# Attention's first steps in a fused kernel: transposes of the first step ahead of the fourth step's scores, and the second pair's keys and queries loaded in two parts

## The chip, the cores and the metric

The kernel runs on one core of a Trainium2 chip. The metric is the device time of one execution in microseconds (us), the median of three timed runs. Everything below that is read from a trace comes from one profiled execution of the same program.

## What is computed

Attention over 2 batches, 8 heads, 768 positions and 64 columns per head, with a local window of 96 positions and 8 global ones, and then two feed-forward layers over the 1536 tokens. In the reference:

```python
scores = scale * np.matmul(q, k.transpose(0, 1, 3, 2)) + bias       # bias: -slope of the head * distance
scores = np.where(is_global | is_local, scores, -1000000000.0)
a = np.exp(scores - np.max(scores, axis=-1, keepdims=True))
a = a / (np.sum(a, axis=-1, keepdims=True) + 1e-09)
x = np.matmul(a, v)                  # laid out as 1536 tokens x 512
h = x @ w_in;  x = (h * np.tanh(softplus(h))) @ w_out               # first layer, 512 -> 2048 -> 512
h = x @ w_in2; return gate(h) @ w_out2                              # second layer, another gate
```

## The kernel before

Only attention's beginning is touched. `attention_windows` treats two heads at a time: a pair `(b, p)` is batch `b`, heads `2p` and `2p + 1`. Its keys `kr` (one copy of the window's keys per block of positions, `KB` = 144 columns each), queries `qr` and values `vr` are whole tiles in SBUF, loaded by `load_qk` and `load_v`. A pair has three steps of 256 positions each (`u` = 0 and 1 are the two blocks of 128); 8 pairs make `NU` = 24 steps, numbered `s` over all pairs. So steps 0, 1, 2 belong to pair (0,0) and steps 3, 4, 5 to pair (0,1), whose tiles are `kr01`, `qr01` and `vr01`.

One step is this chain: `scores(s)` on TensorE (PE), `softmax(s, u)` on VectorE (DVE: bias and maximum) and ScalarE (ACT: exponential and row sum), `normalise(s)` on DVE (two small operations) and GpSimd (POOL: four multiplications), `transposes(s)` on PE, `evict(s, 0)` on ACT and `evict(s, 1)` on DVE, which copy the transposed probabilities from PSUM, and `values(s)` on PE. The scores of odd and even steps lie in different PSUM banks, so `scores(s + 2)` can only begin when `softmax(s)` has read its banks.

The order on each engine is written by hand, and every engine runs its instructions in that order. The loop, once per `s`, software-pipelines the chain: in one turn PE gets `scores(s + 1)`, `transposes(s - 2)`, `values(s - 3)`, while DVE and ACT work on `softmax(s, 0)`, `normalise(s - 1)`, `evict(s - 2, 0)`, `softmax(s, 1)` and `evict(s - 2, 1)`. PE's turn for `s = 2` is thus `scores(3)` and then `transposes(0)`.

The loads stand in one queue, issued by the SyncE (SP) in the order of the code. Pair (0,0)'s keys and queries come ahead of everything, in two parts: the first 288 columns of the keys (`K0`) and 256 of the queries (`Q0`), which is what step 0 needs, and then the rest. Behind them come, in the version before, the whole of `kr01` and `qr01`, then `vr00`, `kr02`, `qr02`, `vr01`, `vr02`, and later pairs and weights. Each load has one of eight semaphores in turn, and an issue waits for the load that had that semaphore before, which is the one eight loads earlier.

Of the kernel before, what the change touches and what calls it, by code (L numbers as in the profile page):

```python
# [45 lines left out]
def attention_then_two_ffn_kernel(  # L46
# [29 lines left out]
    def half(j):  # L76
        return slice(j * D, (j + 1) * D)

    Q0, K0 = 2 * P, 2 * KB

    def load_qk(pool, b, p):

        kr = pool.tile([P, NB * KB], F32, tag="kr", name=f"kr{b}{p}")
        qr = pool.tile([P, S], F32, tag="qr", name=f"qr{b}{p}")
        if (b, p) == (0, 0):

            for cols in (slice(0, K0), slice(K0, NB * KB)):
                for j in range(2):
                    nc.sync.dma_start(kr[half(j), cols], k[b, p, half(j), j, cols])
                if cols.start == 0:  # L90
                    nc.sync.dma_start(qr[:, 0:Q0], q[b, p, :, 0:Q0])
            nc.sync.dma_start(qr[:, Q0:], q[b, p, :, Q0:])
        else:
            for j in range(2):
                nc.sync.dma_start(kr[half(j)], k[b, p, half(j), j])
            nc.sync.dma_start(qr, q[b, p])
        raws[b, p] = (qr, kr)

    def load_v(pool, b, p):
        vr = pool.tile([P, NSL, 2, D], F32, tag="vr", name=f"vr{b}{p}")  # L100
        nc.sync.dma_start(vr, v[b, p])
        return vr
# [5 lines left out]
    nc.sync.dma_start(raw, counts.partition_broadcast(P))  # L108
    first = ctx.enter_context(tc.tile_pool(name="first", bufs=1))
    load_qk(first, 0, 0)  # L110
    nc.scalar.preload_act_table_set("natural_log_exp_and_others")
    WU = 2 * DM
# [55 lines left out]
    def rounded(on, to, src):  # L168
        if on == "a":
            nc.scalar.activation(to, src, AF.Copy)  # L170
        else:
            (nc.vector if on == "v" else nc.gpsimd).tensor_copy(to, src)  # L172

    def remainder(on, to, src, hi):
        (nc.vector if on == "v" else nc.gpsimd).tensor_tensor(to, src, hi.bitcast(F32), op=ALU.subtract)  # L175
# [129 lines left out]
    def attention_windows(x_hi, x_lo, bank, wts, opening):  # L305
        with ExitStack() as es:
            cp = es.enter_context(tc.tile_pool(name="a_const", bufs=1))
            rp = es.enter_context(tc.tile_pool(name="a_raw", bufs=3))
            pp = es.enter_context(tc.tile_pool(name="a_p", bufs=2))
            sp = es.enter_context(tc.tile_pool(name="a_s", bufs=3))  # L310
            vs = {}
            for p in range(3):
                if p < 2:
                    load_qk(rp, 0, p + 1)
                vs[0, p] = load_v(rp, 0, p)
            bias = cp.tile([P, H, 3 * P], F32, name="bias")

# [16 lines left out]
            NU = len(steps)  # L334
# [3 lines left out]
            def scores(s):  # L338
                b, p, t = steps[s]
                qr, kr = raws[b, p]  # L340
                scs[s] = [bank(SC[s % 2][j], [2, 2 * P]) for j in range(2)]
                for u in range(2):
                    i = 2 * t + u
                    for j, ps in enumerate(scs[s]):
                        nc.tensor.matmul(ps[:, u, 0:keys(i)], qr[half(j), i * P:(i + 1) * P],  # L345
                                         kr[half(j), window(i):window(i) + keys(i)], start=True, stop=True)

            def softmax(s, u):
                b, p, t = steps[s]
                if u == 0:  # L350
                    probs[s] = (pp.tile([P, 2, 2, 2 * P], F32, tag="pr", name=f"pr{s}", bufs=3),
                                sp.tile([P, 2, 2, 4], F32, tag="st", name=f"st{s}", bufs=3))
                pr, st = probs[s]
                n = keys(2 * t + u)
                for j, ps in enumerate(scs[s]):
                    h = 2 * p + j
                    nc.vector.tensor_tensor_reduce(  # L357
                        pr[:, u, j, 0:n], ps[:, u, 0:n], bias[:, h, 0:n] if n > P else bias[:, h, 2 * P:],
                        scale=-scale, scalar=3e38, op0=ALU.add, op1=ALU.min,
                        accum_out=st[:, u, j, 0:1],  # L360
                    )
                    nc.scalar.activation(pr[:, u, j, 0:n], pr[:, u, j, 0:n], AF.Exp, scale=-1.0,  # L362
                                         bias=st[:, u, j, 0:1], accum_out=st[:, u, j, 1:2])

            def normalise(s):
                pr, st = probs[s]
                nc.vector.tensor_scalar(st[..., 2], st[..., 1], 1e-9, None, op0=ALU.add)
                nc.vector.reciprocal(st[..., 3], st[..., 2])  # L368
                for u in range(2):
                    n = keys(2 * steps[s][2] + u)  # L370
                    for j in range(2):
                        nc.gpsimd.tensor_scalar(pr[:, u, j, 0:n], pr[:, u, j, 0:n], st[:, u, j, 3:4], 1.0,  # L372
                                                op0=ALU.mult, op1=ALU.mult)

            def blocks(s):

                t = steps[s][2]
                return [(u, j, o) for u in range(2) for j in range(2) for o in range(keys(2 * t + u) // P)]

            def transposes(s):  # L380

                pr = probs.pop(s)[0]
                pts[s] = (pp.tile([P, 8, P], F32, tag="pts", name=f"pts{s}"), [bank(TR[c], [8, D]) for c in range(2)])
                for n, (u, j, o) in enumerate(blocks(s)):
                    for c, pt in enumerate(pts[s][1]):
                        nc.tensor.transpose(pt[:, n], pr[half(c), u, j, o * P:(o + 1) * P], ident[half(c), half(c)])  # L386

            def evict(s, c):
                n = len(blocks(s))
                dst, src = pts[s]  # L390
                rounded("av"[c], dst[:, 0:n, half(c)], src[c][:, 0:n])

            def values(s):
                b, p, t = steps[s]
                vr = vs[b, p]
                src = pts.pop(s)[0]
                place = {x: n for n, x in enumerate(blocks(s))}
                for u in range(2):
                    i = 2 * t + u
                    g, (t0, n) = [(g, x) for g, x in enumerate(pieces) if x[0] <= i * P < x[0] + x[1]][0]  # L400
                    pv = bank(PV[g], [n])
                    m = keys(i) // P
                    for o in range(m):
                        for j in range(2):
                            nc.tensor.matmul(pv[half(j), i * P - t0:(i + 1) * P - t0], vr[:, 2 * i - m + 1 + o, j],  # L405
                                             src[:, place[u, j, o]], start=(o == 0), stop=(o == m - 1))
                    if (i + 1) * P == t0 + n:
                        done.append((x_hi[b][:, p, t0:t0 + n], x_lo[b][:, p, t0:t0 + n], pv))
# [3 lines left out]
            for s in range(-1, NU + 4):  # L412

                if s in (3, 7):
                    wts.load()
                if s >= 2 and s % 3 == 2 and s // 3 + 3 < len(pairs):
                    load_qk(rp, *pairs[s // 3 + 3])
                if s >= 6 and s % 3 == 0 and s // 3 + 1 < len(pairs):
                    vs[pairs[s // 3 + 1]] = load_v(rp, *pairs[s // 3 + 1])
                ready, done[:] = done[:], []  # L420
                for hi, lo, src in ready:
                    rounded("a", hi, src)
                if s + 1 < NU:
                    scores(s + 1)
                if 0 <= s - 2 < NU:
                    transposes(s - 2)
                if 0 <= s - 3 < NU:
                    values(s - 3)
                if 0 <= s < NU:
                    softmax(s, 0)  # L430
                if 0 <= s - 1 < NU:
                    normalise(s - 1)
                for hi, lo, src in ready:
                    remainder("v", lo, src, hi)
                if 0 <= s - 2 < NU:
                    evict(s - 2, 0)
                if 0 <= s < NU:
                    softmax(s, 1)
                if 0 <= s - 2 < NU:
                    evict(s - 2, 1)  # L440
                for name in BESIDE.get(s, ()):
                    opening[name]()
                    if name in ("V01", "V11"):
                        wts.load()
# [612 lines left out]
    with tc.If(few != 0) as cmp:  # L1057
        arm(attention_windows, True)
# [53 lines left out]
```

## Time and profile before

| | |
|---|---|
| median of three runs | 603.69 us (603.65 to 604.11) |
| the profiled execution | 604.59 us |
| its span, first to last instruction | 602.8 us |
| PE busy | 585.0 us (97%) |
| DVE busy | 464.4 us (77%) |
| ACT busy | 398.5 us (66%) |
| attention's steps, about | 5 to 80 us of the span |

The span is what the trace shows; 1.79 us of the profiled execution lie outside it. The shares of busy time are means over attention and the two layers, which have different limits: in attention PE, DVE and ACT are all nearly full, in the layers PE alone is. The change lies wholly in the span's first 20 us. Times below are counted from the span's start.

### The profile page before, as it was taken

To read this page: it belongs to the slowest core of one execution; us is meant where nothing else is said; L and a number is where in the kernel's file an instruction comes from. 1 tells how busy PE (TensorE), PEld (TensorE's weight loads), DVE (VectorE), ACT (ScalarE), POOL (GpSimd) and SP (SyncE) were. 2 spreads that over 40 slices of the span, in tenths; PEclk is the share of its full clock that TensorE was granted. 3 is DMA by queue.
4 is the path that set the end of the run, shared out by engine and by line. 5 is a ranking of instruction groups with operands and counts; after the bars stand their busy time and mean duration, and the time that the engine had idled before them with its cause. 6 is when DMAs were issued, how large, how long until landed. Compare 5 with 4: busy or idle time off the path is not lost.

```text
span 602.8 us, 9716 instructions
## 1 busy us (share of the span) xinstructions
PE 585.0 (97%) x3536; PEld 512.4 (85%) x3536; DVE 464.4 (77%) x1036; ACT 398.5 (66%) x872; POOL 67.3 (11%) x146
## 2 busy tenths in 40 slices
PE   5998999999999999999999999999999999999996
PEld 3887789999999999999999888878888888888884
DVE  6999998888888676776767774988688787787571
ACT  4999978888888566677766876667464643544240
POOL 3776710000000000000000000000020140200000
PEclk9999999999999999999999999999999999999998
DMA  7998024433334202221535566510042270310012
GB/s 197 297 272 247 32 71 140 140 103 114 134 141 139 71 1 70 71 82 60 183 114 192 152 194 214 149 61 2 0 126 84 64 216 1 111 29 0 1 47 99
DMA packets 17335, 66.64 MB, mean 111 GB/s; under 512 B 2176, under 2 KB 2432, under 8 KB 13184
## 3 DMA queue, kind: packets, MB, share of 16 engines
q1 hardware_dynamic: 11808, 55.98, 29.6%
q0 software_dynamic: 4608, 8.39, 4.9%
q10 hardware_dynamic: 864, 1.57, 0.7%
q8 instruction: 30, 0.49, 0.3%
q14 instruction: 25, 0.20, 0.1%
HBM read 54.40 MB, written 11.53 MB: 109 GB/s over the span
## 4 chain that ended last, share of the span: by engine, by line
PE 87%; DVE 7%; ACT 3%; DMA 1%; SPq 1%; issue 0%; POOL 0%; DVEq 0%
PE psum L591 22%; PE psum L895 14%; PE psum L805 13%; PE psum L541 10%; PE psum L542 10%; PE psum L544 10%; PE psum L600 7%; DVE pr L357 2%; ACT pr L362 2%; PE psum L345 1%; DVE pts L172 1%; DVE x_lo L175 1%; PE psum L386 1%; PE psum L405 1%; DMA qr<-in_q_dram 1%
## 5 line engine op out<-in xcount | busy, mean ns | idle before, releaser
L541 PE MATMUL psum<-x_hi,whi 128*128 128x384 f32 (+1 forms) x320 | 111.2, 348 | 0.4 <-DVE kr L558 0.4
L542 PE MATMUL psum<-x_lo,whi 128*128 128x384 f32 (+1 forms) x320 | 110.6, 346 | 0.0
L591 PE MATMUL psum<-g_lo,whi 128*128 128x512 f32 (+1 forms) x256 | 86.6, 338 | 0.1
L591 PE MATMUL psum<-g_hi,wlo 128*128 128x512 f32 (+1 forms) x256 | 86.2, 337 | 0.0
L591 PE MATMUL psum<-g_hi,whi 128*128 128x512 f32 (+1 forms) x256 | 86.1, 336 | 0.0
L544 PE MATMUL psum<-x_hi,wlo 128*128 128x384 f32 (+1 forms) x320 | 71.8, 345 | 0.0
L541 PEld LDWEIGHTS psum<-x_hi,whi 128*128 128x128 f32 x320 | 60.2, 188 | 3.7 <-DVE kr L558 0.6
L170 ACT ACTIVATE whi<-wbits 128x512 fp32r<-128x512 f32 x72 | 44.5, 618 | 27.6 <-DVE wbits L758 14.1
L542 PEld LDWEIGHTS psum<-x_lo,whi 128*128 128x128 f32 x320 | 60.2, 188 | 2.4
L544 PEld LDWEIGHTS psum<-x_hi,wlo 128*128 128x128 f32 x320 | 57.3, 188 | 2.5
L175 DVE TENSOR_TENSOR wlo<-wbits,whi 128x512 fp32r<-128x512 f32 x76 | 51.9, 689 | 9.2 <-ACT whi L170 9.1
L731 POOL DMA_DIRECT2D whi<-kept_hi x16 | 8.7, 541 | 430.4 <-ACT room_lo L844 362.5
L591 PEld LDWEIGHTS psum<-g_lo,whi 128*128 128x128 f32 x256 | 48.2, 188 | 5.8 <-DVE g_lo L580 0.5
L591 PEld LDWEIGHTS psum<-g_hi,whi 128*128 128x128 f32 x256 | 48.2, 188 | 5.7
L591 PEld LDWEIGHTS psum<-g_hi,wlo 128*128 128x128 f32 x256 | 48.1, 188 | 5.7
L362 ACT ACTIVATE pr<-pr,st 128x256 f32<-128x256 f32 (+1 forms) x96 | 46.0, 482 | 8.4 <-DVE st L357 8.2
L227 ACT ACTIVATE wbits<-stage 128x512 uint16<-128x512 uint16 x64 | 50.0, 782 | 0.7 <-DVE wlo L175 0.7
L372 POOL TENSOR_SCALAR pr<-pr,st 128x256 f32<-128x256 f32 (+1 forms) x96 | 44.4, 480 | 27.9 <-DVE st L368 14.4
L234 DVE SCALAR_TENSOR_TENSOR wbits<-wsc,wbits 128x512 uint32<-128x512 uint32 x60 | 41.5, 691 | 6.8 <-ACT wbits L227 2.5
L345 PE MATMUL psum<-kr,qr 64*128 64x256 f32 (+1 forms) x192 | 31.3, 413 | 10.8 <-DVE wsc L151 5.3
L162 ACT ACTIVATE wsc<-stage 128x512 f32<-128x512 f32 x60 | 39.6, 660 | 0.0
L357 DVE CUSTOM_DVE_ANT_0 pr<-psum,bias 128x256 f32<-128x256 f32 (+1 forms) x96 | 34.0, 393 | 1.2 <-PE psum L345 1.2
(158 smaller groups left out, 1284.3 us busy)
## 6 DMA issues: line engine op xcount, KB each, us to landing
stage<-in_w_dram SPq DMA_DIRECT2D x32, 1024.0 KB, 5.0
vr<-in_v_dram SPq DMA_DIRECT2D x8, 704.0 KB, 10.7
kept_hi<-whi SPq DMA_DIRECT2D x8, 512.0 KB, 7.2
kept_lo<-wlo SPq DMA_DIRECT2D x8, 512.0 KB, 8.0
whi<-kept_hi POOLq DMA_DIRECT2D x16, 256.0 KB, 3.8
wlo<-kept_lo POOLq DMA_DIRECT2D x16, 256.0 KB, 3.9
kr<-in_k_dram SPq DMA_DIRECT2D x14, 216.0 KB, 12.6
qr<-in_q_dram SPq DMA_DIRECT2D x7, 384.0 KB, 11.7
```

The source lines that it names most:

```text
L170: nc.scalar.activation(to, src, AF.Copy)
L175: (nc.vector if on == "v" else nc.gpsimd).tensor_tensor(to, src, hi.bitcast(F32), op=ALU.subtract)
L227: nc.scalar.activation(bits[:, i, :, 0], words(U16, i, 1), AF.Copy, scale=2.0 ** -13, bias=2.0 ** -14 - 0.5)
L357: nc.vector.tensor_tensor_reduce(pr[:, u, j, 0:n], ps[:, u, 0:n], bias[:, h, 0:n] if n > P else bias[:, h, 2 * P:], scale=-scale, scalar=3 ...
L362: nc.scalar.activation(pr[:, u, j, 0:n], pr[:, u, j, 0:n], AF.Exp, scale=-1.0, bias=st[:, u, j, 0:1], accum_out=st[:, u, j, 1:2])
L372: nc.gpsimd.tensor_scalar(pr[:, u, j, 0:n], pr[:, u, j, 0:n], st[:, u, j, 3:4], 1.0, op0=ALU.mult, op1=ALU.mult)
L541: nc.tensor.matmul(ph, wh[:, c], xh[:, c, tok], start=(c == 0), stop=False)
L542: nc.tensor.matmul(ph, wh[:, c], xl[:, c, tok], start=False, stop=False)
L544: nc.tensor.matmul(ph, wl[:, c], xh[:, c, tok], start=False, stop=(c == KD - 1))
L591: nc.tensor.matmul(y, lhs[:, w], rhs[:, t0:t0 + n], start=(f == 0 and i == 0 and c % share == 0), stop=(f == NF - 1 and i == 2 and c % sha ...
L805: nc.tensor.matmul(ps, a[:, cols], x, start=(n == 0), stop=(n == 3 * HK - 1))
L895: nc.tensor.matmul(ys[c], lhs[:, w], rhs, start=(n == 0 and k == 0), stop=(n == len(fs) - 1 and k == 2))
```

## The change

The transposes of step 0 are taken out of their place behind `scores(3)` and issued ahead of it. Pair (0,1)'s keys and queries are loaded in two parts, as the first pair's are: first columns, then `vr00`, then the rest. Nothing is computed otherwise, and no later turn of the loop differs.

```diff
-    def load_qk(pool, b, p):
+    def load_qk(pool, b, p, between=None):
 
         kr = pool.tile([P, NB * KB], F32, tag="kr", name=f"kr{b}{p}")
         qr = pool.tile([P, S], F32, tag="qr", name=f"qr{b}{p}")
-        if (b, p) == (0, 0):
+        if (b, p) == (0, 0) or between:
 
             for cols in (slice(0, K0), slice(K0, NB * KB)):
                 for j in range(2):
                     nc.sync.dma_start(kr[half(j), cols], k[b, p, half(j), j, cols])
                 if cols.start == 0:
                     nc.sync.dma_start(qr[:, 0:Q0], q[b, p, :, 0:Q0])
+                    if between:
+                        between()
             nc.sync.dma_start(qr[:, Q0:], q[b, p, :, Q0:])
...
             vs = {}
-            for p in range(3):
-                if p < 2:
-                    load_qk(rp, 0, p + 1)
+            def first_values():
+                vs[0, 0] = load_v(rp, 0, 0)
+
+            load_qk(rp, 0, 1, first_values)
+            load_qk(rp, 0, 2)
+            for p in range(1, 3):
                 vs[0, p] = load_v(rp, 0, p)
...
                 for hi, lo, src in ready:
                     rounded("a", hi, src)
+                if s == 2:
+                    transposes(0)
                 if s + 1 < NU:
                     scores(s + 1)
-                if 0 <= s - 2 < NU:
+                if 0 < s - 2 < NU:
                     transposes(s - 2)
```

TensorE, in the version before, from the last scores of pair (0,0) on. `kr_68` and `qr_69` are that pair's tiles, `kr_166` and `qr_167` pair (0,1)'s; `pr_193` and `pr_207` are the probabilities of steps 0 and 1, and `vr_171` is `vr00`.

```order
L345 MATMUL psum<-kr_68,qr_69 128x256 x10
L345 MATMUL psum<-kr_166,qr_167 128x128 x2
L345 MATMUL psum<-kr_166,qr_167 128x256 x2
L386 MATMUL psum<-ident,pr_193 128x64 x12
L345 MATMUL psum<-kr_166,qr_167 128x256 x4
L386 MATMUL psum<-ident,pr_207 128x64 x16
L405 MATMUL psum<-pts_234,vr_171 64x128 x6
```

The same place with the change (the lines of the code are moved by five; `pr_196` and `pr_210` are the probabilities of steps 0 and 1).

```order
L350 MATMUL psum<-kr_68,qr_69 128x256 x10
L391 MATMUL psum<-ident,pr_196 128x64 x12
L350 MATMUL psum<-kr_166,qr_167 128x128 x2
L350 MATMUL psum<-kr_166,qr_167 128x256 x6
L391 MATMUL psum<-ident,pr_210 128x64 x16
L410 MATMUL psum<-pts_233,vr_171 64x128 x6
```

The twelve transposes of step 0 moved from behind the four products of `scores(3)` to ahead of them, and the four products of `scores(4)` now follow those of `scores(3)` at once.

SyncE's queue of loads, before, from the first load of pair (0,1) on (`kr_173` and `qr_174` are pair (0,2)'s, `vr_178` and `vr_180` are `vr01` and `vr02`).

```order
L95 DMA kr_166<-in_k_dram 64x864 x2
L96 DMA qr_167<-in_q_dram 128x768
L101 DMA vr_171<-in_v_dram 128x1408
L95 DMA kr_173<-in_k_dram 64x864 x2
L96 DMA qr_174<-in_q_dram 128x768
L101 DMA vr_178<-in_v_dram 128x1408
L101 DMA vr_180<-in_v_dram 128x1408
```

The same place with the change (`kr_176` and `qr_177` are pair (0,2)'s now).

```order
L89 DMA kr_166<-in_k_dram 64x288 x2
L91 DMA qr_167<-in_q_dram 128x256
L103 DMA vr_171<-in_v_dram 128x1408
L89 DMA kr_166<-in_k_dram 64x576 x2
L94 DMA qr_167<-in_q_dram 128x512
L97 DMA kr_176<-in_k_dram 64x864 x2
L98 DMA qr_177<-in_q_dram 128x768
```

Three loads became six; the second parts of `kr01` and `qr01` stand behind the 704 KB of `vr00` instead of ahead of them, and `kr02` and all behind it stand three issues later.

## Rows read from the trace of the kernel before

**Rows 1.** The page's head and its first part, TensorE's row.

```profile
span 602.8 us, 9716 instructions
...
PE 585.0 (97%) x3536; PEld 512.4 (85%) x3536; DVE 464.4 (77%) x1036; ACT 398.5 (66%) x872; POOL 67.3 (11%) x146
```

**Rows 2.** Busy time in 16.0 to 25.6 us: PE, PEld, DVE, ACT, POOL, clock, DMA.

```profile
16.00:25.60 9.60, 9.41 (x132) 8.16 (x134) 9.32 (x44) 9.60 (x38) 8.00 (x18) 1.00 1.03 320
```

**Rows 3.** Timeline of PE: start, length, line, tiles, count, idle time before, releaser.

```profile
7.83 3.78 PE L345 MATMUL psum<-kr,qr 64*128 64x256 f32 x16 [0.86 <-DMA qr<-in_q_dram]
12.89 1.02 PE L345 MATMUL psum<-kr,qr 64*128 64x128 f32 x8 [1.28 <-DVE st L367]
...
14.12 1.08 PE L345 MATMUL psum<-kr,qr 64*128 64x256 f32 x7
14.91 0.78 PE L386 MATMUL psum<-ident,pr 64*128 64x64 f32 x16
15.92 0.88 PE L405 MATMUL psum<-pts,vr 128*64 128x128 f32 x12 [0.23 <-DMA vr<-in_v_dram]
16.72 1.27 PE L345 MATMUL psum<-kr,qr 64*128 64x256 f32 x8
17.69 0.85 PE L386 MATMUL psum<-ident,pr 64*128 64x64 f32 x16
...
27.29 0.93 PE L345 MATMUL psum<-kr,qr 64*128 64x128 f32 x8
```

**Rows 4.** Timeline of SP's queue: when each load was issued.

```profile
6.96 0.58 SPq L96 DMA_DIRECT2D qr<-in_q_dram  x1
7.59 0.43 SPq L101 DMA_DIRECT2D vr<-in_v_dram  x1
8.06 1.11 SPq L95 DMA_DIRECT2D kr<-in_k_dram  x2
9.22 1.26 SPq L96 DMA_DIRECT2D qr<-in_q_dram  x1
...
15.89 0.33 SPq L96 DMA_DIRECT2D qr<-in_q_dram  x1
```

**Rows 5.** Loads issued at 2.44, 4.22, 6.96, 7.59, 15.89: KB, us to landing.

```profile
qr<-in_q_dram SPq DMA_DIRECT2D x1, 128.0 KB, 2.4
...
qr<-in_q_dram SPq DMA_DIRECT2D x1, 256.0 KB, 3.5
...
qr<-in_q_dram SPq DMA_DIRECT2D x1, 384.0 KB, 5.8
...
vr<-in_v_dram SPq DMA_DIRECT2D x1, 704.0 KB, 8.3
...
qr<-in_q_dram SPq DMA_DIRECT2D x1, 384.0 KB, 10.5
```

**Rows 6.** Timeline of DVE, 11 to 15 us.

```profile
11.57 0.08 DVE L357 DVE_READ_ACCUMULATOR2_ANT st<- 128x1 f32 x1
...
12.49 0.35 DVE L367 TENSOR_SCALAR st<-st 128x4 f32<-128x4 f32 x1
...
14.31 0.56 DVE L172 COPY pts<-psum 128x384 f32<-128x384 f32 x1 [0.60 <-PE psum L386]
```

**Rows 7.** Timeline of POOL: the last multiplication of step 0, all four of step 1.

```profile
12.34 0.47 POOL L372 TENSOR_SCALAR pr<-pr,st 128x256 f32<-128x256 f32 x1
...
13.28 1.83 POOL L372 TENSOR_SCALAR pr<-pr,st 128x256 f32<-128x256 f32 x4
```

**Rows 8.** Timeline of ACT: evictions of steps 0, 1, 2, and what precedes the first.

```profile
13.67 0.19 ACT L362 ACTIVATION_READ_ACCUMULATOR pr<-pr,st 128x1 f32 x1
14.26 0.49 ACT L170 ACTIVATE pts<-psum 128x384 f32<-128x384 f32 x1 [0.41 <-PE psum L386]
...
16.40 0.58 ACT L170 ACTIVATE pts<-psum 128x512 f32<-128x512 f32 x1
...
18.85 0.58 ACT L170 ACTIVATE pts<-psum 128x512 f32<-128x512 f32 x1
```

## The prediction

> **What bounds the kernel now.** I read the page's head and the busy times first: the span is 602.8 us and TensorE (PE) is busy for 97% of it [rows 1]. That share is a mean over stages, so I went on to the busy time by stretches. From 16.0 to 25.6 us ACT is busy for all 9.60 us, PE for 9.41 and DVE for 9.32, at the full granted clock, and the DMA engines are full too [rows 2]. Nothing has room there: whatever delays one engine at the start of attention is carried along, and whatever frees all three is kept. So the change is worth what it shifts ACT, the fullest, and nothing that it does later can add to it.
>
> Then the timeline of the place. PE stands idle for 1.28 us ahead of `scores(3)`, which begin at 12.89, and the profile puts this down to a DVE operation at 12.49 [rows 3, 6]. I don't believe the name. What `scores(3)` needs of DVE is that it has read the scores of step 1, and that ended with the reading at 11.57 (0.08 long) [rows 6]; the operation at 12.49 is the next step's. The queries of pair (0,1) were issued at 6.96 and landed 5.8 us later, at 12.76 [rows 4, 5], and PE starts 0.13 us after that. It is the same distance as at the first pair: issued at 4.22, 3.5 us to landing, PE at 7.83 [rows 3, 5]. So `scores(3)` wait for a load, and `transposes(0)`, which stand behind them, wait with them. For those transposes ACT is idle for 0.41 us before 14.26 and DVE for 0.60 before 14.31 [rows 6, 8]. A third wait, of 0.23 us at 15.92, is PE's for `vr00`: 7.59 plus 8.3 is 15.89 [rows 3 to 5].
>
> **The change part by part.** All sums are made against the profiled execution (span 602.8, whole 604.59), which is 0.9 us over the median of 603.69; I apply the difference to both.
>
> *Transposes first.* They need step 0's probabilities from POOL, whose last multiplication starts at 12.34 and takes 0.47 us [rows 7], so it ends at 12.81. Twelve transposes cost, by the sixteen that take 0.78 us [rows 3], 0.05 us each; eight of them can go earlier, the last four follow 12.81, and with some 0.2 us for the pipeline they are done at about 13.25. ACT comes free at 13.86 (13.67 + 0.19) [rows 8], DVE at 14.31 - 0.60 = 13.71 [rows 6]. Both find the transposes done. So ACT's 0.41 us and DVE's 0.60 us go away. What is moved costs nothing: PE would have stood idle. `scores(3)` start at about 13.1 instead of 12.89, and this is hidden, as their first reader on DVE stands behind the eviction that takes 13.71 to about 14.2.
>
> *First columns in front.* They are 72 KB twice and 128 KB, and the nearest row, the first pair's 128 KB, landed in 2.4 us [rows 5]: issued at 6.96, here at 9.4. At worst they land with the whole tile at 12.76. Either is ahead of 13.1, when `scores(3)` can first start behind the transposes. So the first part by itself is worth nothing: the transposes have already taken the place of the wait. `vr00` has 544 KB fewer ahead of it and lands at some time before 15.89, which takes up to 0.23 us of PE's wait away.
>
> *The second part behind `vr00`.* This is what is late next. `scores(4)` read columns 176 to 432 of the keys and 256 to 384 of the queries, so they need the second parts, which before lay whole in SBUF at 12.76. Now three issues take the slots at 8.06 to 9.22 that `kr02` and `qr02` had [rows 4], and 544 KB go behind the 704 KB. When does the last of them, issued at 9.22, land? The earliest is its quickest precedent, 256 KB in 3.5 us [rows 5]: 12.7. The latest is 15.89, the landing of `vr00` in the version before, since the bytes in the queue up to there are the same. In between I have no row that decides; both ends are whole precedents, so I take the middle, 14.3.
>
> What it costs follows from the steady turn. From landing to start 0.1 us; `scores` to `transposes` of a turn without waits 17.69 - 16.72 = 0.97; the sixteen transposes 0.79 (16.72 + 0.97 + 0.79 is where the values of that turn begin) [rows 3]. So ACT's eviction of step 1 can begin at landing + 1.86. Before, it began at 16.40 [rows 8], and with ACT 0.41 earlier it would at 15.99. It is therefore early by the full 0.41 when the second part lands by 14.1, and even at 14.54. PE has less room: `values(0)` begin at landing + 1.86 instead of 15.92, and the eviction of step 2, at 18.85 before [rows 8], needs `values(0)`, `scores(5)` and `transposes(2)`, which took from 15.92 to about 18.53 (17.69 + 0.85) [rows 3], a reserve of 0.3 us. So the shift at 18.85 is landing + 1.86 - 15.92 - 0.32, that is landing - 14.38, and no better than -0.41. With 14.3 it is -0.1 us. With 12.7 it is -0.41; with 15.89 it is +1.5.
>
> *What is queued behind.* While `scores(4)` wait, `transposes(1)`, `values(0)` and `scores(5)` wait behind them on PE, and for these ACT and DVE; that is the sum above. On SP, three more issues push `kr02` back by about 1.7 us (0.58 each [rows 4]), but the DMA engines are full, so bytes and not issues set when it lands. An issue also waits for the load eight ahead of it: `vr02` now waits for `vr00`, and the keys of pair (0,3) behind it. Before, its queries were the load that waited for `vr00`, issued at 15.89 and landed 10.5 us later, at 26.4; `scores(9)` used them at 27.29 [rows 3 to 5]. They now wait for the second part of `qr01`, not later than 15.89. Reserve 0.9 us, so nothing.
>
> The sum: -0.41 from the transposes, +0.3 back through `scores(4)`, so about -0.1 us: 604.5 for a profiled execution, 603.6 for the median.
>
> **The rivals.**
>
> *Wholly hidden.* The second part lands by 14.0 and the change gives its 0.41 us, at best the 0.57 that PE can have (`values(0)` from 15.92 to 15.35, POOL's last multiplication of step 1 ending at 13.28 + 1.83 = 15.11 [rows 7]). The median is then 603.1 to 603.3. For it speaks the precedent of 3.5 us; against it, that this one was the last load in a short queue, while now 704 KB lie ahead. The Trainium skill (DMA: Bandwidth & Descriptors, on the two cost components of a transfer) gives about 2.0 us and the bytes at 436 GB/s, which would be an estimate of 2.6 us and a landing at 11.8, hidden with ease; the row of 3.5 us for the same size is already longer, and 5.8 and 8.3 us behind it show that a queue is not in that rule.
>
> *The other side: the second part lands behind all of `vr00`.* For it speaks that the loads of rows 5 landed in the order of issue, 12.76 and then 15.89, each after the bytes ahead of it. If it lands at 15.6 or later, the shift is over +1.2 us and the change is slower; at 15.89 the median is 605.2. Against it, that the second part is small, and that 12.76 to 15.89 held other loads as well. The Trainium skill (same page, on HWDGE ordering) says that each DMA engine takes its descriptors in ring order and that a load is complete only when every engine has done its share; by that the second part cannot pass `vr00`, which the order of the landings bears out.
>
> *The change gains much more.* Over 1.2 us would need all of PE's 1.28 us; POOL's 12.81 and 15.11 forbid it.
>
> *A later load becomes late*, through the eight semaphores or the smaller pieces. Only the reserve of 0.9 us at 27.29 could go, some 0.5 us slower.
>
> **How the numbers follow.** The forecast (landing between 14.0 and 15.0, shift -0.4 to +0.6) has 0.55; wholly hidden 0.25; behind all of `vr00` 0.12, with 15.0 to 15.6 counted to the forecast's side; a later load 0.05; much more 0.03. The likeliest shift is -0.1 us, so 603.6. A measurement of this kernel can tell 0.2% from no change, 1.2 us: only landings after 15.6 reach it on one side, and nothing that I can work out on the other. So faster 0.03, same 0.85, slower 0.12. The range goes from the hidden case with 0.1 us for the spread of the runs, 603.1, to the middle of the late one, 604.9.
>
> **What would show it right or wrong.** Right: `transposes(0)` end at 13.0 to 13.3 and evictions begin at 13.7 to 13.9; `scores(3)` begin at 13.1; ahead of `scores(4)` or behind them PE waits for a `qr` or `kr` load, and this sets the evictions of step 1. The load of 256 KB issued at about 9.2 shows its landing. From 16 us on every engine's rows are shifted by one amount, and the layers behind show none of their own. Wrong: a landing before 13 or after 15.9; an eviction of step 1 that is early although the load was late; a shift that shrinks or grows after 20 us, which would mean that the stretch there is not as full as I read it.

## The result, and the profile after

The change makes the kernel slower: 608.41 us, the median of six runs (607.62 to 609.12), against 604.19 for the version before in the same measurement (603.65 to 606.07); the ratio is 1.0065, 95% interval 1.005 to 1.008. The forecast was 603.6 with a range up to 604.9, so the result lies outside it, on the side that I gave 0.12. The profiled execution of the changed kernel took 609.0 us, the second longest of the six; its span is 607.2, 4.4 more than [rows 1], where the medians differ by 4.2. The code's lines are moved by two to seven: the scores are L350 here, the transposes L391, the values L410, the evictions of ACT L172.

First the head of the page of the changed kernel, and the row of TensorE's clock in 40 slices of the span.

```profile
span 607.2 us, 9720 instructions
...
PEclk9799999999999999999999999999999999999999
```

One slice stands out: in the second, about 15 to 30 us, the granted clock was 0.7 of full speed on average. The same row before had no such slice. Next the timeline of PE in the changed kernel, to be laid beside [rows 3].

```profile
7.44 3.79 PE L350 MATMUL psum<-kr,qr 64*128 64x256 f32 x16 [0.41 <-DMA qr<-in_q_dram]
11.22 1.60 PE L391 MATMUL psum<-ident,pr 64*128 64x64 f32 x12
12.65 0.95 PE L350 MATMUL psum<-kr,qr 64*128 64x128 f32 x8
16.49 2.17 PE L350 MATMUL psum<-kr,qr 64*128 64x256 f32 x8 [2.88 <-DMA qr<-in_q_dram]
18.33 1.18 PE L391 MATMUL psum<-ident,pr 64*128 64x64 f32 x16
19.44 1.55 PE L410 MATMUL psum<-pts,vr 128*64 128x128 f32 x12
20.91 1.66 PE L350 MATMUL psum<-kr,qr 64*128 64x256 f32 x8
22.41 0.66 PE L391 MATMUL psum<-ident,pr 64*128 64x64 f32 x16
```

`transposes(0)` and `scores(3)` are where I put them, a little earlier still. Then PE stands idle for 2.88 us ahead of `scores(4)`, for a load of queries. The load is the 256 KB of `qr01`'s second part; its issue in SP's queue:

```profile
9.22 0.59 SPq L94 DMA_DIRECT2D qr<-in_q_dram  x1
```

and from the DMA issues of these windows what the values (issued at 7.58) and this second part took from issue to landing:

```profile
vr<-in_v_dram SPq DMA_DIRECT2D x1, 704.0 KB, 5.7
...
qr<-in_q_dram SPq DMA_DIRECT2D x1, 256.0 KB, 7.1
```

The values landed at 13.28, earlier than before (15.89, [rows 4, 5]), and the second part at 16.36 by the chain of waits (9.22 and 7.14): later than either end of my bounds. The busy times of the changed kernel by stretches (PE, PEld, DVE, ACT, POOL, granted clock, DMA share, GB/s):

```profile
13.40:15.00 1.60, 0.21 (x2) 0.00 (x0) 0.96 (x6) 1.60 (x7) 1.33 (x3) 1.00 1.09 196
15.00:16.40 1.40, 0.00 (x0) 0.00 (x0) 0.87 (x6) 0.59 (x4) 0.99 (x3) 0.57 1.02 209
16.40:21.60 5.20, 5.11 (x40) 4.53 (x42) 1.89 (x8) 2.15 (x8) 1.34 (x3) 0.50 1.05 345
21.60:24.00 2.40, 2.40 (x40) 2.00 (x36) 1.36 (x6) 1.24 (x4) 2.12 (x5) 0.91 0.99 180
```

While PE waited, its clock fell from 2.4 to 1.2 GHz, at about 15.2 us, and it stayed there until about 22.0 (0.91 as the mean of the last row), through nearly all of the work that had been waiting. The same view of 8 to 16 us in one stretch, first of the changed kernel, then of the one before:

```profile
8.00:16.00 8.00, 5.39 (x36) 3.53 (x32) 6.30 (x37) 7.39 (x30) 4.53 (x11) 0.95 1.02 240
```

```profile
8.00:16.00 8.00, 6.50 (x62) 5.24 (x64) 5.49 (x31) 6.93 (x28) 3.92 (x9) 1.00 1.00 269
```

The DMA engines are as full in both, and move less in the changed kernel. And the evictions of ACT, of steps 0 to 3, beside [rows 8]:

```profile
13.37 0.47 ACT L172 ACTIVATE pts<-psum 128x384 f32<-128x384 f32 x1
19.45 0.60 ACT L172 ACTIVATE pts<-psum 128x512 f32<-128x512 f32 x1 [3.86 <-PE psum L391]
...
23.16 0.60 ACT L172 ACTIVATE pts<-psum 128x512 f32<-128x512 f32 x1 [1.16 <-PE psum L391]
...
26.10 0.48 ACT L172 ACTIVATE pts<-psum 128x384 f32<-128x384 f32 x1
```

Step 0's eviction is 0.89 us earlier than before, step 1's 3.05 later, step 2's 4.31 later. From there on nothing changes: the span ends 4.4 later. Of the 0.89 us, 0.39 has nothing to do with the order of the transposes: PE began the products ahead of them at 7.44, and at 7.83 in [rows 3], as the first pair's load landed sooner. In the traces of the other kernels below, the two with whole keys and queries among them, PE begins there between 7.39 and 7.66, and once at 7.92; the one trace of the version before is a late one, and every early shift against it below is flattered by some 0.2 to 0.4 us.

**Where the 4.4 us lie.** My own formula, landing - 14.38, gives +1.98 us for a landing at 16.36. What is left is the clock, read as distances between PE's starts, after against [rows 3]: `scores(4)` to `transposes(1)` 1.84 against 0.97, `transposes(1)` to `values(0)` 1.11 against 0.79, `values(0)` to `scores(5)` 1.47 against 0.80, `scores(5)` to `transposes(2)` 1.50 against 0.97. That is 2.39 us more. 1.98 and 2.39 make 4.37, and the eviction of step 2 is 4.31 late. So the theory to be tested is: the second part is late because the 704 KB of the values are ahead of it; this costs about 2 us; and the wait halves PE's clock, which costs as much again. Rivals: the transposes' new place has a price; cutting the tiles slows the loads whatever the order; the clock is a bystander.

This split is that of the profiled execution. Each run lists its mean granted clock over the span: four of the six, 608.04 to 609.12 us, have 0.992 or 0.993, as the profiled one, but the two shortest have 0.996 (607.68 us) and 0.998 (607.62 us), and the version before 0.997 in its trace. The 6.8 us at half clock (15.2 to 22.0) take 0.0056 off the mean, so the run of 607.62 us cannot hold such a fall; it is 3.4 us over before's median all the same, and has no trace.

### The profile page after: what moved, and what is told of

It is laid out like the page before. It is cut to its first block, busy times and chain, and to the rows that moved or that the text cites. A ratio compares the mean times of both kernels' runs of the same rounds, so it can differ in the third digit from the quotient of the medians.

```text
span 607.2 us, 9720 instructions
## 1 busy us (share of the span) xinstructions
PE 588.4 (97%) x3536; PEld 514.5 (85%) x3536; DVE 464.9 (77%) x1036; ACT 398.9 (66%) x872; POOL 67.6 (11%) x146
## 4 chain that ended last, share of the span: by engine, by line
PE 86%; DVE 7%; ACT 2%; DMA 2%; SPq 1%; issue 0%; POOL 0%; DVEq 0%; ACTq 0%
PE psum L598 21%; PE psum L902 14%; PE psum L812 13%; PE psum L548 10%; PE psum L549 9%; PE psum L551 9%; PE psum L607 7%; DVE pr L362 2%; ACT pr L367 1%; DMA qr<-in_q_dram 1%; DVE pts L174 1%; PE psum L350 1%; DVE x_lo L177 1%; PE psum L391 1%; PE psum L410 1%
## 5 line engine op out<-in xcount | busy, mean ns | idle before, releaser
L172 ACT ACTIVATE whi<-wbits 128x512 fp32r<-128x512 f32 x72 | 44.6, 619 | 27.6 <-DVE wbits L765 14.1
L350 PE MATMUL psum<-kr,qr 64*128 64x256 f32 (+1 forms) x192 | 32.6, 431 | 11.8 <-DVE wsc L153 5.4
L350 PEld LDWEIGHTS psum<-kr,qr 64*128 64x128 f32 x192 | 21.3, 213 | 17.8 <-DVE st L362 9.6
```

## The experiments

The lines' numbers differ a little from kernel to kernel. All ratios are to the version before, measured on the same chip with it.

**One half alone: the transposes, with the loads of the version before.**

```diff
+                if s == 2:
+                    transposes(0)
                 if s + 1 < NU:
                     scores(s + 1)
-                if 0 <= s - 2 < NU:
+                if 0 < s - 2 < NU:
                     transposes(s - 2)
```

> The loads are those of the version before; only the transposes of step 0 stand ahead of scores(3). Theory (the loads' second part is the whole loss): ACT evicts step 0 at 13.8 instead of 14.26, scores(4) wait for nothing, PE's idle time at 15.9 for the values remains and takes some of it back: 0.2 to 0.4 us faster than before, a ratio of 0.9993 to 0.9997. Rival (moving the transposes costs something by itself): 1 us or more slower than before.

Measured: 604.16 us against 604.54, ratio 0.9992 (0.9981 to 1.0002); span 601.9. Its timeline of PE and of ACT:

```profile
12.81 1.86 PE L345 MATMUL psum<-kr,qr 64*128 64x128 f32 x16
...
16.16 0.88 PE L405 MATMUL psum<-pts,vr 128*64 128x128 f32 x12 [0.90 <-DMA vr<-in_v_dram]
```

```profile
15.66 0.57 ACT L170 ACTIVATE pts<-psum 128x512 f32<-128x512 f32 x1
18.69 0.60 ACT L170 ACTIVATE pts<-psum 128x512 f32<-128x512 f32 x1 [0.49 <-PE psum L386]
```

`scores(3)` and `scores(4)` run in one piece, step 1 is evicted 0.74 us earlier than before (0.22 of it by the earlier start, 7.61 against 7.83), and then PE waits 0.90 us for the values and step 2 is only 0.16 us early. The transposes' new place shows no price. That it is a gain is not shown, as the interval holds 1.

**The other half alone: the parts, with the transposes behind `scores(3)` again.**

```diff
-                if s == 2:
-                    transposes(0)
                 if s + 1 < NU:
                     scores(s + 1)
-                if 0 < s - 2 < NU:
+                if 0 <= s - 2 < NU:
                     transposes(s - 2)
```

> The loads in parts as in the changed kernel, but the transposes of step 0 behind scores(3) again. Theory (the second part behind the values is the whole loss, the transposes' place has no share in it): scores(3) begin at 11.7 instead of 12.9, PE waits about 3 us for the second part, the clock falls to half for some 5 us, and the time is 3.5 to 5 us over before's, as the changed kernel. Rival (the new place of the transposes opens PE's idle time and so the loss): within 1 us of before.

Measured: 607.61 against 604.59, ratio 1.0055 (1.0037 to 1.0073); span 607.0. PE's wait in its timeline, and the stretch behind it:

```profile
16.32 2.17 PE L350 MATMUL psum<-kr,qr 64*128 64x256 f32 x8 [3.52 <-DMA qr<-in_q_dram]
```

```profile
16.30:21.30 5.00, 4.99 (x38) 4.43 (x40) 1.76 (x8) 2.02 (x8) 1.40 (x4) 0.50 1.02 327
```

The loads alone bring the wait, the halved clock and the loss. The profiled span is 4.2 us over before's; the median is 3.0 over, less than the 3.5 that I expected at the least and than the changed kernel's 4.2, but the two intervals overlap, so no share of the transposes is shown.

**The wait filled.** The changed kernel with useless products on PE behind `scores(3)`.

```diff
                 if s + 1 < NU:
                     scores(s + 1)
+                if s == 2:
+                    for _ in range(3):
+                        nc.tensor.matmul(bank(PV[0], [TT]), ident, other[:, 0:TT], start=True, stop=True)
```

> The changed kernel with three additional products of 128 x 512 on PE behind scores(3), about 0.86 us each, whose result nothing reads. They fill the time in which PE waited for the second part. Theory (the halved clock is over half of the loss): the second part lands at 16.4 as before, but the clock stays at 1.0, scores(4) to transposes(1) take 1.8 us instead of 3.0, ACT evicts step 1 at 18.2 instead of 19.45 and step 2 at 20.8 instead of 23.16, and the time is 1.6 to 2.2 us over before's, about 606. Rival (the clock is a bystander; the wait alone does it): 4 us over before's, as the changed kernel.

Measured: the profiled span is 604.6, 1.8 over before's, as the theory said; but of six runs two took 606.5 and four 607.8 to 608.4, so the median is 607.96 and the ratio 1.0056 (1.0044 to 1.0068), which fits the rival. The trace is of the shortest of the six (606.45 us): PE, the stretches, ACT.

```profile
13.60 2.84 PE L434 MATMUL psum<-kr,ident 128*128 128x512 f32 x6
16.37 1.14 PE L350 MATMUL psum<-kr,qr 64*128 64x256 f32 x8
```

```profile
13.40:16.40 3.00, 3.00 (x11) 1.09 (x8) 1.90 (x11) 2.26 (x11) 2.32 (x7) 1.00 1.06 206
16.40:21.60 5.20, 5.20 (x81) 4.45 (x82) 3.30 (x15) 3.57 (x13) 2.81 (x8) 1.00 1.04 356
```

```profile
18.03 0.60 ACT L172 ACTIVATE pts<-psum 128x512 f32<-128x512 f32 x1 [2.37 <-PE psum L391]
20.49 0.58 ACT L172 ACTIVATE pts<-psum 128x512 f32<-128x512 f32 x1
```

`scores(4)` begin at 16.37, where they began in the changed kernel too (16.49), but at full clock, and step 2 is evicted at 20.49 instead of 23.16. The load was not the same: it landed at 15.5 here (9.22 and 6.3), and it is the filling that holds `scores(4)` until then. But the start is the same within 0.12 us, so between these two executions the clock makes about 2.5 us of the 2.67 at step 2, and as much of the 2.6 in the span. What the four longer runs were was open, so I ran this kernel three times more.

> The filled wait once more, as two of its six runs took 606.5 us and four about 608. Theory: in the slow ones the second part landed after the filling had ended, PE waited again and the clock fell; an execution of about 608 shows a granted clock of 0.5 behind 16.4, one of 606.5 doesn't. Rival: the slow ones wait at a later load, with the clock at 1.0 until 24 us.

> As the repetition before it: about 608 with the clock halved behind 16.4, or about 606.5 with the clock at 1.0; the rival is a later load's wait at the full clock.

> As the repetitions before it: about 608 with the clock halved behind 16.4, or about 606.5 with the clock at 1.0; the rival is a later load's wait at the full clock.

Measured: spans 604.9, 604.9 and 606.0 (606.80, 606.81 and 607.87 us). The first two hold the clock at 1.00 throughout. The third is one of the longer; its PE, and its stretch from 12.5 us:

```profile
7.39 2.89 PE L350 MATMUL psum<-kr,qr 64*128 64x256 f32 x16 [0.42 <-DMA qr<-in_q_dram]
11.13 0.62 PE L391 MATMUL psum<-ident,pr 64*128 64x64 f32 x4 [0.85 <-POOL pr L377]
...
14.21 3.75 PE L434 MATMUL psum<-kr,ident 128*128 128x512 f32 x6
```

```profile
12.50:15.40 2.90, 2.90 (x14) 1.73 (x15) 2.32 (x13) 2.90 (x13) 2.22 (x6) 0.52 1.06 199
```

Its clock was halved as well, but from about 12.6 us on, ahead of the filling, which then took 3.75 us instead of 2.84 and ended at 17.96, well after the load (9.2 and 6.9: 16.1). So for this execution neither theory nor rival had the place right: it is one of half clock, yet not behind a second wait. The second repetition, one of the short ones, speaks against the theory too: there PE did wait 0.29 us for the load behind the filling, and the clock held.

The four longer runs of the first measurement are hardly of this kind. Each lists a mean granted clock of 0.998, as the two shorter ones do (0.998 and 0.997), where the third repetition lists 0.995. What made them 1.4 to 1.9 us longer stays open; a later load's wait at the full clock, the rival, would fit, but none was seen in a trace of this kernel. So the clock's share is shown between traced executions; the medians, 607.96 against the changed kernel's 608.41, do not show it.

**Filled beyond the landing.** The same with five products instead of three.

> As the filled wait, with five additional products instead of three: they end at about 18.2, nearly 2 us after the second part landed, so scores(4) are later than in the changed kernel (16.5). Theory (half clock is over half of the changed kernel's loss): the clock stays at 1.0, ACT evicts step 1 at 20.0, and the profiled execution is 3.3 to 3.9 us over before's, no slower than the changed kernel although PE does 4.6 us of useless work. Rival (start of scores(4) alone decides): 1.7 us slower than the changed kernel.

Measured: span 606.3, 3.5 over before's; 608.01 against 604.59, ratio 1.0062 (1.0049 to 1.0075), no slower than the changed kernel's 1.0065 (1.005 to 1.008). The stretch of the filling, `scores(4)` behind it, and step 1 on ACT:

```profile
13.40:18.10 4.70, 4.70 (x15) 1.87 (x12) 1.85 (x11) 2.21 (x10) 3.67 (x8) 1.00 1.03 222
```

```profile
18.05 1.14 PE L350 MATMUL psum<-kr,qr 64*128 64x256 f32 x8
```

```profile
19.70 0.60 ACT L172 ACTIVATE pts<-psum 128x512 f32<-128x512 f32 x1 [4.09 <-PE psum L391]
```

`scores(4)` start 1.6 us later than in the changed kernel, and the kernel ends 0.9 us earlier. Start alone does not decide; the clock is no bystander. Here the medians say so as well: all six runs (607.83 to 608.61 us) list a clock of 0.998 or 0.999. And my formula, which knows no clock, fits: for a landing 0.1 us ahead of 18.05 it gives +3.6, and the span has +3.5.

**The wait taken away, the loads left as they are.**

```diff
-                    i = 2 * t + u
+                    i = 2 * t + u if s != 4 else 1
```

> The changed kernel, but scores(4) read the first part's columns (the second block's) for both of its blocks, so the scores of step 4 are not the reference's; the amount of work is the same. No instruction needs the second part before scores(5). Theory: PE does not wait at scores(4), the clock stays at 1.0, scores(5) need the second part at about 16.3 and wait for it a few tenths at most: 0.4 us faster to 0.4 us slower than before. Rival (the three more loads slow the whole queue and something else waits): 2 us or more slower than before.

Measured: 604.17 against 604.54, ratio 0.9993 (0.9984 to 1.0003). Without the wait at `scores(4)` the loss is gone, although all six loads stand where the change put them. The profiled execution took 606.11 us, more than the median, and shows another wait:

```profile
16.94 1.25 PE L350 MATMUL psum<-kr,qr 64*128 64x256 f32 x8 [0.55 <-DMA qr<-in_q_dram]
...
29.60 1.02 PE L350 MATMUL psum<-kr,qr 64*128 64x128 f32 x8 [2.34 <-DVE x_lo L177]
```

`scores(5)` wait 0.55 us for the second part, about as expected. `scores(9)` wait 2.34 us; the name is DVE's, but these are the first scores of pair (0,3), and that pair's queries, issued at 16.82, took 12.6 us and so landed at 29.4, 0.2 us ahead of 29.60: I take it for that load. It is my rival of the later load; it did not reach the median.

**The order of the parts.** The second parts ahead of the values.

```diff
-                    if between:
-                        between()
             nc.sync.dma_start(qr[:, Q0:], q[b, p, :, Q0:])
+            if between:
+                between()
```

> The six pieces are kept, but the values come behind the second part instead of ahead of it. Theory: with 704 KB fewer ahead of it the last second part lands at 11.5 to 13.5 instead of 16.4, scores(4) don't wait, the clock stays at 1.0, and the time is 0.2 to 0.5 us under before's. Rival (the loss comes of cutting the tiles, whatever the order): the second part still lands after 15 and the time is 2 us or more over before's.

Measured: 605.48 against 604.54, ratio 1.0019 (1.001 to 1.0028), slower, where I expected a small gain. The second part (issued at 8.75) and the values (at 9.38), PE, and the stretches:

```profile
qr<-in_q_dram SPq DMA_DIRECT2D x1, 256.0 KB, 3.2
...
vr<-in_v_dram SPq DMA_DIRECT2D x1, 704.0 KB, 7.6
```

```profile
17.00 1.31 PE L410 MATMUL psum<-pts,vr 128*64 128x128 f32 x12 [1.72 <-DMA vr<-in_v_dram]
18.24 2.08 PE L350 MATMUL psum<-kr,qr 64*128 64x256 f32 x8
```

```profile
15.30:17.00 1.70, 0.00 (x0) 0.00 (x0) 1.70 (x9) 1.70 (x7) 1.44 (x4) 1.00 1.03 250
17.00:20.60 3.60, 3.60 (x30) 2.81 (x32) 1.28 (x8) 1.19 (x6) 2.98 (x7) 0.54 1.01 346
```

The second part lands at 11.95, as the theory said, and `scores(4)` wait for nothing. Now the values come late instead, at 16.98, PE waits 1.72 us for them, and the same thing happens one step further on: half clock, from about 17.3 us, just after the wait. A wait was moved, not removed. The trace is of the longest of the eleven runs (607.39 us); the median is 0.9 us over before's, and most of the other runs list a mean clock of 0.997 to 0.999, so they cannot be taken to show the same fall.

**Fewer values between.** The changed kernel with 192 KB of `vr00`, which is what step 0 needs, between the parts.

```diff
             def first_values():
-                vs[0, 0] = load_v(rp, 0, 0)
+                vs[0, 0] = rp.tile([P, NSL, 2, D], F32, tag="vr", name="vr00")
+                nc.sync.dma_start(vs[0, 0][:, 0:3], v[0, 0, :, 0:3])
 
             load_qk(rp, 0, 1, first_values)
+            nc.sync.dma_start(vs[0, 0][:, 3:], v[0, 0, :, 3:])
```

> The changed kernel with 192 KB of vr00 (the slices that step 0 needs) between the first and the second parts instead of all 704 KB; the other 512 KB follow behind the second part. Theory (the bytes ahead of the second part set its landing): it lands at 12.5 to 14, PE waits less than 1 us at scores(4), the clock stays at 1.0, and the time is between 0.5 us faster and 0.5 us slower than before. Rival (six and more small loads slow the queue whatever stands between): landing after 15.5, clock halved, 3 us or more slower.

Measured: 604.55 against 604.12, ratio 1.0003 (0.9993 to 1.0013); span 602.3. The second part, issued at 9.22:

```profile
qr<-in_q_dram SPq DMA_DIRECT2D x1, 256.0 KB, 3.9
```

It took 3.9 us, where it took 7.1 behind 704 KB, PE waited for no load of pair (0,1) or of a later one, and the clock held. Cutting the tiles is not what costs; the bytes ahead are.

**The second part from another queue.** Its three loads issued by ACT's queue instead of SP's.

```diff
+                queue = nc.scalar if between and cols.start else nc.sync
                 for j in range(2):
-                    nc.sync.dma_start(kr[half(j), cols], k[b, p, half(j), j, cols])
+                    queue.dma_start(kr[half(j), cols], k[b, p, half(j), j, cols])
...
-            nc.sync.dma_start(qr[:, Q0:], q[b, p, :, Q0:])
+            queue.dma_start(qr[:, Q0:], q[b, p, :, Q0:])
```

> The changed kernel, but the three loads of the second part are issued from ScalarE's queue, beside SyncE's queue with the values, and not behind it. Theory (what delays the second part is the 704 KB of the values ahead of it in one queue): it lands at 11 to 14, the values some later than 13.3, and no wait at scores(4); 0.5 us faster to 1 us slower than before, as the values may now be late. Rival (the loads are slow because the DMA engines are full, whichever queue they stand in): the second part still lands after 15.5 and the time is 3 us or more over before's.

Measured: 604.88 against 604.59, ratio 1.0003 (0.9993 to 1.0012). The second part (issued by ACT at 6.65), and a stretch:

```profile
qr<-in_q_dram ACTq DMA_DIRECT2D x1, 256.0 KB, 4.7
```

```profile
13.00:14.00 1.00, 1.00 (x9) 1.00 (x8) 0.72 (x3) 1.00 (x4) 1.00 (x3) 0.50 1.02 274
```

It lands at 11.35, beside the values and not behind them, and the 4 us are gone. (It is issued 2.6 us earlier than in the changed kernel, and takes 4.7 us instead of 7.1.) In this execution PE's clock was halved from about 12.7 to 16.1 us, without a wait for any load: the same early fall as in the longer one of the filled kernels.

**The best of the parts.** Transposes ahead, keys and queries whole as before, `vr00` in two loads, the three slices of step 0 first.

```diff
-        nc.sync.dma_start(vr, v[b, p])
+        for rows in ((slice(0, 3), slice(3, NSL)) if (b, p) == (0, 0) and pool is not first else (slice(0, NSL),)):
+            nc.sync.dma_start(vr[:, rows], v[b, p, :, rows])
```

> Transposes ahead, keys and queries whole as before, and vr00 in two loads: the three slices that step 0 needs (192 KB) and then the other eight. Theory: PE's wait of 0.9 us for the values goes, as 192 KB land by about 14; 0.2 to 0.6 us faster than before, a ratio of 0.9990 to 0.9997, at or below that of the transposes alone. Rival (every extra piece slows the queue, as in the changed kernel): a later load becomes late and it is no faster than before.

Measured: 604.02 against 604.59, ratio 0.9991 (0.9979 to 1.0002); span 602.4. ACT, steps 1 and 2:

```profile
15.59 0.58 ACT L171 ACTIVATE pts<-psum 128x512 f32<-128x512 f32 x1
18.04 0.58 ACT L171 ACTIVATE pts<-psum 128x512 f32<-128x512 f32 x1
```

All waits for loads in this stretch are gone, and both evictions are 0.81 us earlier than in [rows 8], of which 0.29 is the earlier start of this execution (7.54 against 7.83). The median fits the expectation and its interval still holds 1; a version that beats the one before beyond doubt was not found.

## Why the prediction was wrong

- *What bounds the stretch.* Right for the changed kernel. The wait at `scores(3)` was the load and not DVE's operation, and a shift made there is kept: +4.31 us at step 2 in the changed kernel and +4.4 at the end, +1.64 and +1.8 in the filled one. In the two shortest spans (the transposes alone, the best of the parts) the end differs more from step 2's shift: -0.16 and -0.9, -0.81 and -0.4. A shift that grows or shrinks was my sign of a wrong reading; why it does there stays open.
- *Transposes first.* Right. Step 0's eviction follows ACT's work without a pause (13.37 after, against 14.26); without the earlier start of this execution that is 0.50 us, where I had 0.41. Alone the move shows no cost.
- *First columns in front.* Right: `scores(3)` did not wait for them.
- *Second part behind `vr00`: the step that failed first.* I put the landing between 12.7 and 15.89 and took the middle, 14.3. It was 16.36, and with that my formula gives a median of 605.7 (603.69 and 1.98), outside the range before any clock comes in. The upper end assumed that the same bytes need the same time; but in the changed kernel the DMA engines, as full as before, moved 240 GB/s from 8 to 16 us where they had moved 269. That the pieces are the reason is not shown: in still more pieces, with 192 KB between, it was 260, and 284 with the loads of before in the transposes alone. And the middle had no ground: the order of the landings in [rows 5] spoke for the late end. With 192 KB of values ahead the same load takes 3.9 us, with 704 KB 7.1. (The Trainium skill's rule for a load by itself, DMA: Bandwidth & Descriptors, on the two cost components, is fitted on loads that GpSimd issues, and these are SyncE's; its estimate of 2.6 us was far off here.) What hangs on this is my formula, which gives +1.98 for 16.36; the filled wait, which keeps all but the clock, measured +1.8 in its shortest execution for a start at 16.37, and the longer filling +3.5 for one at 18.05. The mechanism was the one of my rival *behind all of `vr00`*, and its price for the wait was right. (The columns that I gave for `scores(4)`, 176 to 432 and 256 to 384, are those of the first of its two blocks; the other reads 320 to 576 and 384 to 512, out of the second parts too.)
- *The term that I left out: PE's clock.* I priced the delayed work at the durations of [rows 3], all of which ran at full clock. After the wait it ran at half in the profiled execution, which is 2.39 us by the distances between PE's starts and about 2.5 by the filled wait. There it is larger than the wait's own price, and it takes the time well beyond even the late rival's 605.2. It is not the whole of the rest: the run of 607.62 us is 1.9 over the 605.7 of my formula at a mean clock of 0.998, and whether its load was later still or something else waited stays open. Nothing in the rows of before showed such a fall: its longest wait there, 1.28 us, was followed by full clock. The Trainium skill (TensorE: Matmul & The Clock Gate, on the clock gate) has the two levels, 1.2 and 2.4 GHz, and says that an idle PE is put back to the lower; I had not weighed it, as I asked only what the wait costs the chain. The trace agrees: the clock fell to 0.50 while PE was idle. Not every fall here is of that kind (last section).
- *The eight semaphores.* They did not show in the changed kernel. A late first load of pair (0,3), landing at 29.4 where it was 26.4 before, was seen in one execution, in the kernel without the wait.

## What to carry to other kernels

The wait that the transposes were moved out of did not go when loads were put back; it went to the next consumer of what was late, from `scores(3)` to `scores(4)` and, with the order of the parts turned, to the values. So list who needs the bytes that are put back, and when, before those that are put forward. Take the landing of a load from the bytes ahead of it in its queue, at the late end where the queue is full. And price a new wait of PE twice: what it holds up, and the clock at which the held work then runs; filling it with useless products tells the two apart, if single executions are compared by their traces and by the mean clock that each run lists, as a median mixes executions that lost their time in different ways.

## What was not expected of the hardware

PE's granted clock fell within the waits of 2.88 us (the changed kernel) and 3.52 us (the parts alone), and just after one of 1.72 us (the parts turned), but not behind the 1.28 us of the version before or the 0.90 of the transposes alone. It was back at full only after some 5.5 us of work at half clock in the changed kernel and after 3.4 us with the parts turned. In two executions (ACT's queue and the third repetition of the filled wait) it fell at about 12.7 us with no load waited for: in both, the sixteen products from 7.4 us on had taken 2.9 us, PE then stood idle for 0.85, and short pieces of transposes followed. In the changed kernel these products took 3.8 us and left no such gap. The record shows a clock of 1.00 for them in either case, so why they take 2.9 or 3.8 us stays open, and so does whether this has a part in the spread between runs of one kernel (2.4 us in six runs of the version before).
